# P times V on four quarters of the array, results in the free halves of the score banks, a third accumulator for the feed-forward product, and routing with eight wider matmuls

## Chip, cores and metric

The kernel runs on one core of one Trainium2 chip. The metric is the device time of one execution in microseconds (us); the time before is the median of three runs.

## The reference

Three stages follow one another on 4608 tokens of width 512. Everything is float32, and the kernel keeps that accuracy by splitting each operand into a high and a low float16 half and adding three products (high·high, high·low, low·high).

```
# attention in chunks of 64, 8 heads of width 64
scores = q_c @ k_c.T / sqrt(64);  attn = softmax(scores);  x = attn @ v_c
# dense feed-forward, 512 -> 2048 -> 512
h = relu(x @ w_in);  x = (h * h) @ w_out
# 8 experts, top 1: the router picks one expert for each token
logits = x @ w_gate + modality_bias[modality_id];  e = argmax(logits)
gate = softmax(logits)[e];  out = gate * (relu(x @ w1[e]) @ w2[e])
```

## The kernel before

Tokens are cut into 36 tiles of 128, and four tiles make a super (nine supers). A tile of attention runs through `attn_split` (halves of q and k), `attn_s` (scores, TensorE), `attn_max` (VectorE), `attn_exp` (ScalarE), `attn_p`, `attn_psplit`, `attn_ptr` (a transposing DMA), `attn_pv` (P times V, TensorE), `attn_x` (the result is split into `xt`, its high half on ScalarE, its low half on VectorE), `x_sq` and `x_norm`. For each super, sixteen steps `mm1` (12 matmuls of 512 columns each, into a PSUM tile `hp`) and sixteen steps `mm2` (12 such matmuls, into `op`) follow. ScalarE takes `hp` out as `r`, VectorE squares it to `g`, ScalarE writes the high half of the square into `big`, and GpSimd the low half. After `mm2`, `x2_evac`, `x2_tr`, `route_a` and `route_b` store the row and its expert; the experts' weights are split beside that (`piece_split`). When all tiles are through, slots of 128 rows of one expert each run `slot_mm1` and `slot_mm2`; their rows come by a gather (`slot_gather`) and a transposing DMA (`slot_tr`).

The order on each engine is written by the program itself. For tiles 8 to 35, `attn_events` gives each part of a tile a planned time (`attn_pv` at 36 us of the tile's own plan, `attn_s` at 14, a new tile every 20.5 us of that plan), and `flush` issues what is due before each step of 2.65 planned us; a table `COST` of ScalarE and VectorE time puts parts off when either is too full, and a table `AFTER` holds a part back until an earlier one has been issued. The first 86 us are ordered by `plan_start`, a list of operations with dependencies and due times. Tiles 0 to 3 (`FULL`) multiply in float32 without halves.

PSUM has eight banks: two for `hp` (pool `ps_h`), two for `op`, two for the scores (`s_all`, of which each bank uses columns 0 to 255; at the start `narrow_hi` writes columns 256 to 511 too), one for P times V (`ps_x`) and one for everything small (`ps_r`). In `attn_pv` head half `j` has its operands on partitions 64j, and its result goes to partitions 64j of the one bank:

```
nc.tensor.matmul(xp[h, hp, 64 * c:64 * c + 64], lhsT=vs[h, la, c, hp, :],
                 rhs=pt[h, lb * KD + hp, 64 * c:64 * c + 64], start=n == 0, stop=n == 2)
```

In `attn_s` the four pairs of operand half `j` and result half `c` go to four places: partitions 64c of bank `j`.

`route_a` makes 12 matmuls of 8 columns and VectorE finds the largest logit; ScalarE's exponential of the logits stands at the end of `route_a`, in ScalarE's order ahead of whatever comes next there.

Of the kernel before, what the change touches and what calls it, by code (L numbers as in the profile page):

```python
# [8 lines left out]
F32 = mybir.dt.float32  # L9
F16 = mybir.dt.float16  # L10
# [3 lines left out]
AF = mybir.ActivationFunctionType  # L14
ALU = mybir.AluOpType
# [15 lines left out]
def kernel(  # L31
# [39 lines left out]
    ps_h = ctx.enter_context(tc.tile_pool(name="ps_h", bufs=2, space=bass.MemoryType.PSUM))  # L71
    ps_o = ctx.enter_context(tc.tile_pool(name="ps_o", bufs=2, space=bass.MemoryType.PSUM))
    ps_s = ctx.enter_context(tc.tile_pool(name="ps_s", bufs=1, space=bass.MemoryType.PSUM))
    ps_x = ctx.enter_context(tc.tile_pool(name="ps_x", bufs=1, space=bass.MemoryType.PSUM))
# [35 lines left out]
    wgs = const.tile([128, 2, KD, E], F16, name="wgs")  # L110
# [43 lines left out]
    def consts_c():  # L154
        wg, ids = cb["wg"], cb["ids"]
        act(wgs[:, 0], wg, scale=SWG)
        stt(wgs[:, 1], wg, SWG, wgs[:, 0], ALU.mult, ALU.subtract)
# [31 lines left out]
    s_all = ps_s.tile([128, 2, 512], F32, tag="s", name="s_all")  # L189
    wl = {}  # L190
# [224 lines left out]
    def attn_pv(i):  # L415
        a = at[i]
        pt = a["pt"]
        xp = ps_x.tile([128, KD, 128], F32, tag="x", name="xp")
        a["xp"] = xp
        if i < FULL:  # L420
            for hp in range(KD):
                for c in range(2):
                    for j in range(2):
                        h = slice(64 * j, 64 * j + 64)
                        nc.tensor.matmul(xp[h, hp, 64 * c:64 * c + 64], lhsT=a["vv"][h, c * KD + hp, :],
                                         rhs=pt[h, hp, 64 * c:64 * c + 64], start=True, stop=True)
            return
        vs = a["vs"].rearrange("p l (c h) d -> p l c h d", c=2)
        for hp in range(KD):
            for c in range(2):  # L430
                for n, (la, lb) in enumerate(PASSES):
                    for j in range(2):
                        h = slice(64 * j, 64 * j + 64)
                        nc.tensor.matmul(xp[h, hp, 64 * c:64 * c + 64], lhsT=vs[h, la, c, hp, :],
                                         rhs=pt[h, lb * KD + hp, 64 * c:64 * c + 64], start=n == 0, stop=n == 2)
# [20 lines left out]
    def attn_x(i, part=None):  # L456
        su, t, _, _ = where[i]
        if su not in xts:
            xts[su] = xt_p.tile([128, 2, KD, 512], F16, tag="xt", name="xt")
        a = at[i]  # L460
        x = xts[su]
        sl = slice(t * 128, t * 128 + 128)
        sx = SV if i < FULL else 1.0 / SP_
        if part != 1:
            act(x[:, 0, :, sl], a["xp"], scale=sx)
        if part != 0:
            stt(x[:, 1, :, sl], a["xp"], sx, x[:, 0, :, sl], ALU.mult, ALU.subtract)
# [115 lines left out]
    def route_a(i):  # L583
        a = x2[i]
        lp = ps_r.tile([128, 512], F32, tag="r", name="lp")
        n = 0
        for la, lb in PASSES:
            for kk in range(KD):
                nc.tensor.matmul(lp[:, 0:E], lhsT=a["xt"][:, la * KD + kk, :], rhs=wgs[:, lb, kk, :],
                                 start=n == 0, stop=n == 3 * KD - 1)  # L590
                n += 1
        lg = sm_p.tile([128, E], F32, tag="lg", name="lg")
        stt(lg, lp[:, 0:E], a["ui"][:, 0:1], bias_t[:, i, :], ALU.mult, ALU.add)
        m8 = sm_p.tile([128, 8], F32, tag="m8", name="m8")
# [9 lines left out]
        ex = sm_p.tile([128, E], F32, tag="ex", name="ex")  # L604
        se = sm_p.tile([128, 1], F32, tag="se", name="se")
        act(ex, lg, AF.Exp, bias=nm[:, 0:1], accum_out=se)
        a["oh"], a["se"] = oh, se

    def route_b(i):
# [9 lines left out]
        nc.vector.tensor_tensor(out=run, in0=run, in1=a["oh"], op=ALU.add)  # L619
        mt = sm_p.tile([128, 2], F32, tag="mt", name="mt")  # L620
        nc.gpsimd.tensor_copy(out=mt[:, 0:1], in_=tok[:, i:i + 1])
        ga = sm_p.tile([128, 1], F32, tag="ga", name="ga")
        ts2(ga, a["se"], 1e-9, None, ALU.add)
# [213 lines left out]
    def once(fn, s):  # L837
# [16 lines left out]
        attn_p: (0.0, 1.5), attn_psplit: (0.52, 0.0), attn_x: (0.48, 0.6), x_sq: (0.52, 0.0),  # L854
        x_norm: (0.0, 0.2), piece_split: (0.95, 1.14), x2_evac: (1.2, 1.1), route_a: (0.3, 0.9),
        route_b: (0.0, 0.8),
# [60 lines left out]
    def attn_events(i, a0):  # L917
        more = i + 2 < NTILE
        at_chain([
            (a0 + o, fn, (i + d,)) for o, fn, d in (  # L920
                (0.0, attn_split, 0), (4.5, attn_load, 2), (14.0, attn_s, 0), (16.0, attn_max, 0),
                (18.0, attn_exp, 0), (20.0, attn_p, 0), (23.0, attn_psplit, 0), (23.1, attn_vsplit, 0),
                (26.0, attn_ptr, 0), (27.5, attn_vload, 2), (36.0, attn_pv, 0), (38.0, attn_x, 0), (40.0, x_sq, 0),
                (45.0, x_norm, 0),
            ) if d == 0 or more
        ])
# [5 lines left out]
    def plan_start():  # L932
# [14 lines left out]
        for i in range(FIRST + 2):  # L947
# [14 lines left out]
            else:  # L962
                op(("qh", i), "ACT", 1.05, [("lq", i), ("s", i - 2)], attn_split, i, 0)
                op(("ql", i), "DVE", 1.37, [("qh", i)], attn_split, i, 1)
                op(("s", i), "PE", 0.60, [("ql", i), ("mx", i - 1)], attn_s, i)
# [14 lines left out]
            op(("xh", i), "ACT", 0.60, [("pv", i)], attn_x, i, 0)  # L980
            op(("xl", i), "DVE", 0.69, [("xh", i)], attn_x, i, 1)
# [11 lines left out]
        ops["np", 7][3].append(("onb", KF - 1))  # L993
        op(("cc",), "DVE", 0.60, [("old", KF - 1)], consts_c)
# [79 lines left out]
    for su, (b0, nt, sb) in enumerate(supers):  # L1074
# [7 lines left out]
        for t, qq in M2 if su == 0 else [(t, qq) for t in range(nt) for qq in range(4)]:  # L1082
# [12 lines left out]
            if i == NTILE - 1:  # L1095
                ch += [(T + 12.4, map_b1, ()), (T + 18.4, map_b2, ()), (T + 18.5, once, (slot_w1, EARLY)),
                       (T + 18.6, once, (slot_w2, EARLY)), (T + 21.0, map_b3, ()),
                       (T + 21.1, once, (slot_gather, EARLY)), (T + 21.2, once, (slot_gather, EARLY + 1)),
                       (T + 28.0, once, (slot_tr, EARLY)), (T + 30.0, once, (slot_tr, EARLY + 1))]
# [21 lines left out]
    with tc.manual_schedule():  # L1121
# [3 lines left out]
        for n, (T, fn, a) in enumerate(steps):  # L1125
# [137 lines left out]
```

## Time and profile before

| | |
|---|---|
| median of three runs | 1281.58 us (1281.47 to 1286.59) |
| the profiled execution's own time | 1282.98 us |
| its span, first to last instruction | 1281.3 us |
| TensorE busy | 1232.0 us, 96% of the span |
| VectorE, ScalarE, GpSimd busy | 671.4, 553.8, 409.0 us |
| granted TensorE clock, mean share | 0.989 |

Busy time is time in which at least one instruction of that engine is under way. A matmul's record is longer than the distance to the next one, since they overlap; what a group of matmuls costs TensorE is read from the start of the group to the start of what follows. A bracket in the timeline is the engine's idle time ahead of a row, with what ended it.

### The profile page before, as it was taken

The page shows a single profiled execution, that of the slowest core. Times are in us where ns is not written, and L with a number is a line of the kernel's source. Part 1 is how long each engine was busy: PE and PEld are TensorE (multiplying, and loading weights), DVE is VectorE, ACT ScalarE, POOL GpSimd, SP SyncE. Part 2 cuts the span into 40 slices and gives each one's busy share as a digit, 9 for nine tenths or more (in the row PEclk, how much of TensorE's full clock was granted, in tenths as well). Part 3 has the DMA queues.
Part 4 walks back from the last instruction along what each step waited for, and adds up shares of the span by engine and source line. Part 5 has one row for each costly group of instructions (what it writes and reads, how often), then busy time and mean ns, then how long its engine had stood idle before and what let it go on. Part 6 is the DMA issues. An engine that isn't in the chain of part 4 may idle for free. (4 is left out here: it accounts for less than half of the span.)

```text
span 1281.3 us, 28844 instructions
## 1 busy us (share of the span) xinstructions
PE 1232.0 (96%) x11836; PEld 698.2 (54%) x11836; DVE 671.4 (52%) x1467; ACT 553.8 (43%) x978; POOL 409.0 (32%) x389
## 2 busy tenths in 40 slices
PE   5898999999999999999999999999899999999998
PEld 4443444444444444444444444447677776777775
DVE  6799676796695776776866864514111111111110
ACT  6887564564564554654755653512111111111111
POOL 4487251361350341440531531511222111111111
PEclk8899999999999999999999999999999999999999
DMA  9455536657558458458676553075355337622322
GB/s 375 153 163 167 127 93 188 182 149 218 161 177 218 133 164 223 141 154 217 158 196 175 140 153 111 10 221 164 77 125 102 78 78 259 139 75 75 76 75 59
DMA packets 177867, 190.64 MB, mean 149 GB/s; under 512 B 124876, under 2 KB 124916, under 8 KB 176707
## 3 DMA queue, kind: packets, MB, share of 16 engines
q1 hardware_dynamic: 128930, 157.72, 42.6%
q0 software_dynamic: 7616, 20.80, 5.3%
q10 hardware_dynamic: 41184, 10.23, 4.9%
q8 instruction: 94, 1.54, 0.5%
q14 instruction: 43, 0.34, 0.1%
HBM read 241.02 MB, written 53.08 MB: 230 GB/s over the span
## 5 line engine op out<-in xcount | busy, mean ns | idle before, releaser
L544 PE MATMUL hp<-xt,big 128*128 128x512 f16 x1728 | 388.5, 381 | 9.4 <-ACT r L87 9.2
L559 PE MATMUL op<-big,big 128*128 128x512 f16 x1728 | 384.0, 380 | 0.5 <-POOL big L524 0.5
L544 PEld LDWEIGHTS <-big 128*128 128x128 f16 x1728 | 164.3, 98 | 200.5 <-issue 14.9
L559 PEld LDWEIGHTS <-big 128*128 128x128 f16 x1728 | 165.0, 98 | 193.7 <-issue 1.5
L524 POOL TENSOR_TENSOR big<-g,big 128x512 f16<-128x512 f32 x144 | 176.2, 1227 | 211.9 <-DVE g L90 148.5
L90 DVE SCALAR_TENSOR_TENSOR ht<-hp,ht 128x512 f16<-128x512 f32 x74 | 51.2, 692 | 331.0 <-ACT ht L87 331.0
L812 PEld LDWEIGHTS <-big 128*128 128x128 f16 x3552 | 204.3, 99 | 16.0 <-issue 4.3
L826 PE MATMUL op<-big,ht 128*128 128x512 f16 x888 | 197.6, 379 | 0.0
L812 PE MATMUL hp<-big,big 128*128 128x128 f16 x3168 | 185.5, 221 | 7.4 <-DMA big<-big 3.8
L90 DVE SCALAR_TENSOR_TENSOR g<-r,bq 128x512 f32<-128x512 f32 x138 | 136.4, 993 | 31.7 <-ACT r L87 30.6
L826 PEld LDWEIGHTS <-ht 128*128 128x128 f16 x888 | 85.2, 98 | 96.2
L90 DVE SCALAR_TENSOR_TENSOR wss<-wst,wss 128x1024 f16<-128x1024 f32 x64 | 91.0, 1421 | 62.4 <-ACT wss L87 61.9
L832 POOL DMA_INDIRECT out_dram<-o,tib x33 | 33.5, 1014 | 269.7 <-ACT o L87 250.9
L87 ACT ACTIVATE ht<-hp 128x512 f16<-128x512 f32 x74 | 44.2, 597 | 155.8 <-PE hp L812 155.7
L626 POOL DMA_INDIRECT meta<-mt,di x36 | 41.0, 1138 | 213.5 <-issue 80.8
L87 ACT ACTIVATE big<-r,bls 128x512 f16<-128x512 f32 x138 | 99.4, 721 | 6.4 <-DVE bli L96 0.7
L87 ACT ACTIVATE r<-hp 128x512 f32<-128x512 f32 x138 | 80.9, 586 | 49.3 <-PE hp L544 31.9
L87 ACT ACTIVATE wss<-wst 128x1024 f16<-128x1024 f32 x64 | 67.0, 1047 | 57.2 <-DMA wsp<-wss 39.5
L87 ACT ACTIVATE o<-op,fsb 128x512 f32<-128x512 f32 x33 | 22.7, 687 | 153.3 <-PE op L826 153.3
L407 POOL TENSOR_TENSOR ps<-ee,ps 128x512 f16<-128x512 f32 x32 | 44.1, 1380 | 89.4 <-ACT ps L87 88.0
L87 ACT ACTIVATE ex<-lg,nm 128x8 f32<-128x8 f32 x36 | 10.8, 301 | 116.2 <-DVE nm L94 116.2
L90 DVE SCALAR_TENSOR_TENSOR qkt<-qk,qkt 128x1024 f16<-128x1024 f32 x32 | 44.3, 1383 | 12.8 <-ACT qkt L87 12.0
(175 smaller groups left out, 1008.1 us busy)
## 6 DMA issues: line engine op xcount, KB each, us to landing
big<-wsp SPq DMA_DIRECT2D x72, 2048.0 KB
wst<-in_w_dram SPq DMA_DIRECT2D x64, 512.0 KB
wsp<-wss SPq DMA_DIRECT2D x64, 512.0 KB
qk<-in_qk_dram SPq DMA_DIRECT2D x36, 512.0 KB
vv<-in_v_dram SPq DMA_DIRECT2D x36, 256.0 KB
x2d<-xs SPq DMA_DIRECT2D x36, 256.0 KB
big<-in_w_in_dram SPq DMA_DIRECT2D x16, 512.0 KB
wl<-in_w_out_dram SPq DMA_DIRECT2D x16, 512.0 KB
```

What stands on the lines that cost most here:

```text
L87: nc.scalar.activation(out=out, in_=in_, func=func, **kw)
L90: nc.vector.scalar_tensor_tensor(out=out, in0=in0, scalar=s, in1=in1, op0=op0, op1=op1, **kw)
L407: nc.gpsimd.tensor_tensor(out=a["ps"][:, 1], in0=pf, in1=a["ps"][:, 0], op=ALU.subtract)
L524: nc.gpsimd.tensor_tensor(out=lo, in0=q32.rearrange("p (f n) -> p f n", f=nf), in1=hi, op=ALU.subtract)
L544: nc.tensor.matmul(hp[:, q_ * n:(q_ + 1) * n], lhsT=wi[:, la, kk, f * 128:f * 128 + 128], rhs=x[:, lb, kk, :], start=i == 0, stop=i == 3 * ...
L559: nc.tensor.matmul(ps, lhsT=g[:, la, f, t * 128:t * 128 + 128], rhs=wo[:, lb, f, :], start=f == 0 and n == 0, stop=f == KF - 1 and n == 2)
L626: nc.gpsimd.indirect_dma_start(out=meta[:, :], out_offset=bass.IndirectOffsetOnAxis(ap=di[:, 0:1].bitcast(U32), axis=0), in_=mt, in_offset ...
L812: nc.tensor.matmul(hp[:, f4 * 128:f4 * 128 + 128], lhsT=w[:, la, kk, f * 128:f * 128 + 128], rhs=xt[:, lb * KD + kk, :], start=n == 0, sto ...
L826: nc.tensor.matmul(ps, lhsT=ht[:, la, f, :], rhs=w[:, lb, f, :], start=f == 0 and n == 0, stop=f == KF2 - 1 and n == 2)
L832: nc.gpsimd.indirect_dma_start(out=out[:, :], out_offset=bass.IndirectOffsetOnAxis(ap=slot[s][0].bitcast(U32), axis=0), in_=o, in_offset=N ...
```

## The change

- `attn_pv` for tiles 4 to 35 puts its result into columns 256 to 511 of the score banks: operand half `j` into bank `j`, result half `c` on partitions 64c, with `c` and `j` as the inner loops, so that the four quarters of the array take turns. Tiles 0 to 3 take a buffer of `ps_h` instead of `ps_x`.
- The bank of `ps_x` goes to `ps_h`, which has three buffers; `mm1` may have three results waiting instead of two.
- `attn_x` takes the four quarters out one by one: four instructions on ScalarE and four on VectorE of 64 partitions by 256 elements, in place of one and one of 128 by 512.
- `route_a` makes 8 matmuls of 16 columns (high and low half of the weights side by side, so that the product low·low is added too) and VectorE adds the two halves of the logits in two instructions. The exponential moves to `route_b`, between VectorE's instructions there.
- In the order: `attn_pv` 36 to 43, `attn_x` 38 to 45.5, `x_sq` 40 to 48, `x_norm` 45 to 51; the costs of `attn_x` and the routing; in the start plan, `s(i)` waits for the low half of tile i−2's result and `pv(i)` for the maximum of tile i+1. `slot_tr` for the first two slots after the early ones comes 4 us earlier in its chain.

```diff
-    ps_h = ctx.enter_context(tc.tile_pool(name="ps_h", bufs=2, space=bass.MemoryType.PSUM))
+    ps_h = ctx.enter_context(tc.tile_pool(name="ps_h", bufs=3, space=bass.MemoryType.PSUM))
...
-    ps_x = ctx.enter_context(tc.tile_pool(name="ps_x", bufs=1, space=bass.MemoryType.PSUM))
...
+    xps = [s_all[:, c, 256:512].rearrange("p (h n) -> p h n", h=KD) for c in range(2)]
...
-            for c in range(2):
-                for n, (la, lb) in enumerate(PASSES):
+            for n, (la, lb) in enumerate(PASSES):
+                for c in range(2):
                     for j in range(2):
                         h = slice(64 * j, 64 * j + 64)
-                        nc.tensor.matmul(xp[h, hp, 64 * c:64 * c + 64], lhsT=vs[h, la, c, hp, :],
+                        o = 64 * c
+                        nc.tensor.matmul(xps[j][o:o + 64, hp, :], lhsT=vs[h, la, c, hp, :],
                                          rhs=pt[h, lb * KD + hp, 64 * c:64 * c + 64], start=n == 0, stop=n == 2)
...
+        for j in range(2):
+            for c in range(2):
+                sl = slice(t * 128 + 64 * c, t * 128 + 64 * c + 64)
+                xp, h = xps[j][64 * c:64 * c + 64], slice(64 * j, 64 * j + 64)
+                if part != 1:
+                    act(x[h, 0, :, sl], xp, scale=1.0 / SP_)
+                if part != 0:
+                    stt(x[h, 1, :, sl], xp, 1.0 / SP_, x[h, 0, :, sl], ALU.mult, ALU.subtract)
...
-        n = 0
-        for la, lb in PASSES:
-            for kk in range(KD):
-                nc.tensor.matmul(lp[:, 0:E], lhsT=a["xt"][:, la * KD + kk, :], rhs=wgs[:, lb, kk, :],
-                                 start=n == 0, stop=n == 3 * KD - 1)
-                n += 1
+        for kk in range(2 * KD):
+            nc.tensor.matmul(lp[:, 0:2 * E], lhsT=a["xt"][:, kk, :], rhs=wgs[:, kk % KD].rearrange("p l e -> p (l e)"),
+                             start=kk == 0, stop=kk == 2 * KD - 1)
         lg = sm_p.tile([128, E], F32, tag="lg", name="lg")
         stt(lg, lp[:, 0:E], a["ui"][:, 0:1], bias_t[:, i, :], ALU.mult, ALU.add)
+        stt(lg, lp[:, E:2 * E], a["ui"][:, 0:1], lg, ALU.mult, ALU.add)
...
-        act(ex, lg, AF.Exp, bias=nm[:, 0:1], accum_out=se)
-        a["oh"], a["se"] = oh, se
+        a["oh"], a["nm"], a["lg"] = oh, nm, lg
...
         nc.vector.tensor_tensor(out=run, in0=run, in1=a["oh"], op=ALU.add)
...
+        act(ex, a["lg"], AF.Exp, bias=a["nm"][:, 0:1], accum_out=se)
...
-        ts2(ga, a["se"], 1e-9, None, ALU.add)
+        ts2(ga, se, 1e-9, None, ALU.add)
...
-        attn_p: (0.0, 1.5), attn_psplit: (0.52, 0.0), attn_x: (0.48, 0.6), x_sq: (0.52, 0.0),
+        attn_p: (0.0, 1.5), attn_psplit: (0.52, 0.0), attn_x: (1.4, 1.5), x_sq: (0.52, 0.0),
...
-                (26.0, attn_ptr, 0), (27.5, attn_vload, 2), (36.0, attn_pv, 0), (38.0, attn_x, 0), (40.0, x_sq, 0),
-                (45.0, x_norm, 0),
+                (26.0, attn_ptr, 0), (27.5, attn_vload, 2), (43.0, attn_pv, 0), (45.5, attn_x, 0), (48.0, x_sq, 0),
+                (51.0, x_norm, 0),
...
-                op(("s", i), "PE", 0.60, [("ql", i), ("mx", i - 1)], attn_s, i)
+                op(("s", i), "PE", 0.60, [("ql", i), ("mx", i - 1), ("xl", i - 2)], attn_s, i)
...
+        for i in range(FULL, FIRST - 1):
+            ops["pv", i][3].append(("mx", i + 1))
...
-                       (T + 28.0, once, (slot_tr, EARLY)), (T + 30.0, once, (slot_tr, EARLY + 1))]
+                       (T + 24.0, once, (slot_tr, EARLY)), (T + 26.0, once, (slot_tr, EARLY + 1))]
...
-            while (fn is mm1 and len(pend) == 2) or (pend and fn is mm2 and (a[0] or a[1] < 2)) or any(x not in done for x in need):
+            while (fn is mm1 and len(pend) == 3) or (pend and fn is mm2 and (a[0] or a[1] < 2)) or any(x not in done for x in need):
```

## Rows read from the trace of the kernel before

**Rows 1.** The page's part 1: busy us, share of the span, instructions.

```profile
PE 1232.0 (96%) x11836; PEld 698.2 (54%) x11836; DVE 671.4 (52%) x1467; ACT 553.8 (43%) x978; POOL 409.0 (32%) x389
```

**Rows 2.** Waits of TensorE, whole span: us in total, times, longest us.

```profile
PE hp L544 <- ACT r L87: 9.2, 10, 1.9
...
PE hp L812 <- DMA big<-big: 3.8, 1, 3.8
...
PE xp L434 <- DVE xt L90: 3.1, 1, 3.1
...
PE xp L434 <- issue: 2.5, 1, 2.5
```

**Rows 3.** Groups by form, TensorE: xcount | busy us, mean ns | idle.

```profile
L434 PE MATMUL xp<-pt,vs 64*64 64x64 f16 x1536 | 30.7, 195 | 5.7 <-DVE xt L90 3.1 <-issue 2.5
...
L353 PE MATMUL s_all<-qkt 64*64 64x64 f16 x1536 | 18.6, 195 | 0.3 <-DVE ee L366 0.3
```

**Rows 4.** Timeline of TensorE, 350 to 372 us: start, us, what.

```profile
358.97 0.94 PE L434 MATMUL xp<-pt,vs 64*64 64x64 f16 x48
359.85 2.76 PE L544 MATMUL hp<-xt,big 128*128 128x512 f16 x12
...
370.36 0.58 PE L353 MATMUL s_all<-qkt 64*64 64x64 f16 x48
370.87 1.47 PE L544 MATMUL hp<-xt,big 128*128 128x512 f16 x6
```

**Rows 5.** Timeline of TensorE, 422 to 448 us.

```profile
430.25 0.45 PE L589 MATMUL lp<-wgs,x2t 128*128 128x8 f16 x12
430.56 2.75 PE L544 MATMUL hp<-xt,big 128*128 128x512 f16 x12
435.17 2.75 PE L544 MATMUL hp<-xt,big 128*128 128x512 f16 x12 [1.86 <-ACT r L87]
```

**Rows 6.** Timeline of ScalarE, 422 to 448 us.

```profile
434.24 0.30 ACT L87 ACTIVATE ex<-lg,nm 128x8 f32<-128x8 f32 x1 [5.03 <-DVE nm L94]
...
434.54 0.57 ACT L87 ACTIVATE r<-hp 128x512 f32<-128x512 f32 x1
```

**Rows 7.** Timeline of TensorE, 860 to 925 us: two slots' first product.

```profile
901.27 5.54 PE L812 MATMUL hp<-xgt,big 128*128 128x128 f16 x96
...
915.80 7.15 PE L812 MATMUL hp<-big,big 128*128 128x128 f16 x96 [3.82 <-DMA big<-big]
```

**Rows 8.** Timeline of ScalarE and its DMA issues, 872 to 925 us.

```profile
912.07 0.69 ACT L87 ACTIVATE o<-op,fsa 128x512 f32<-128x512 f32 x1 [4.63 <-PE op L826]
912.40 2.75 ACTq L797 DMA_TRANSPOSE big<-big  x2
```

**Rows 9.** Timeline of GpSimd in the same stretch: the second slot's gather.

```profile
904.75 0.97 POOL L785 DMA_INDIRECT big<-x2d,tib  x1 [0.30 <-issue]
```

**Rows 10.** Groups by form, ScalarE.

```profile
L87 ACT ACTIVATE xt<-xp 128x512 f16<-128x512 f32 x36 | 20.9, 582 | 5.5 <-PE xp L434 5.1 <-PE xp L425 0.4
...
L87 ACT ACTIVATE wgs<-wg 128x32 f16<-128x32 f32 x1 | 0.2, 218 | 0.0
```

**Rows 11.** Groups by form, VectorE.

```profile
L90 DVE SCALAR_TENSOR_TENSOR xt<-xp,xt 128x512 f16<-128x512 f32 x36 | 24.6, 684 | 5.2 <-ACT xt L87 5.2
...
L90 DVE SCALAR_TENSOR_TENSOR lg<-lp,ui,bias_t 128x8 f32<-128x8 f32 x36 | 8.0, 221 | 16.2 <-PE lp L589 16.2
```

**Rows 12.** Timeline of all engines, 0 to 45 us: a score matmul.

```profile
14.24 1.13 PE L345 MATMUL s_all<-qk 64*64 64x64 f32 x32 [2.59 <-DVE big L90]
```

**Rows 13.** Busy time by stretch: PE, PEld, DVE, ACT, POOL, clock, DMA.

```profile
80.00:130.00 50.00, 43.44 (x462) 21.33 (x461) 47.13 (x68) 39.13 (x72) 40.51 (x34) 0.98 0.58 174
...
200.00:760.00 560.00, 551.61 (x4982) 266.34 (x4981) 407.48 (x875) 308.98 (x543) 190.95 (x169) 1.00 0.64 176
```

**Rows 14.** Timeline of VectorE, 358 to 379 us.

```profile
365.65 0.68 DVE L90 SCALAR_TENSOR_TENSOR xt<-xp,xt 128x512 f16<-128x512 f32 x1
...
376.55 0.69 DVE L366 TENSOR_TENSOR ee<-s_all,mx 128x512 f32<-128x512 f32 x1
```

More of the change, by code (lines that the diff above doesn't have):

```diff
@@ L109 @@
     run = const.tile([128, E], F16, name="run")
-    wgs = const.tile([128, 2, KD, E], F16, name="wgs")
+    wgs = const.tile([128, KD, 2, E], F16, name="wgs")
     wnorm = const.tile([128, 1], F32, name="wnorm")
@@ L155, in consts_c @@
         wg, ids = cb["wg"], cb["ids"]
-        act(wgs[:, 0], wg, scale=SWG)
-        stt(wgs[:, 1], wg, SWG, wgs[:, 0], ALU.mult, ALU.subtract)
+        act(wgs[:, :, 0], wg, scale=SWG)
+        stt(wgs[:, :, 1], wg, SWG, wgs[:, :, 0], ALU.mult, ALU.subtract)
         idf = st_p.tile([128, 2 * DM], F16, tag="xs", name="idf", bufs=4)[:NTILE, 0:256].bitcast(F32)
@@ L417, in attn_pv @@
         pt = a["pt"]
-        xp = ps_x.tile([128, KD, 128], F32, tag="x", name="xp")
-        a["xp"] = xp
         if i < FULL:
+            xp = ps_h.tile([128, 512], F32, tag="h", name="xp").rearrange("p (k n) -> p k n", k=KD)
+            a["xp"] = xp
             for hp in range(KD):
@@ L462, in attn_x @@
         sl = slice(t * 128, t * 128 + 128)
[L463 to L467, printed above, removed]
+        if i < FULL:
+            if part != 1:
+                act(x[:, 0, :, sl], a["xp"], scale=SV)
+            if part != 0:
+                stt(x[:, 1, :, sl], a["xp"], SV, x[:, 0, :, sl], ALU.mult, ALU.subtract)
+            return
+        for j in range(2):
+            for c in range(2):
+                sl = slice(t * 128 + 64 * c, t * 128 + 64 * c + 64)
+                xp, h = xps[j][64 * c:64 * c + 64], slice(64 * j, 64 * j + 64)
+                if part != 1:
+                    act(x[h, 0, :, sl], xp, scale=1.0 / SP_)
+                if part != 0:
+                    stt(x[h, 1, :, sl], xp, 1.0 / SP_, x[h, 0, :, sl], ALU.mult, ALU.subtract)
     def x_sq(i):
@@ L603, in route_a @@
         ts2(nm, m8[:, 0:1], -1.0, None, ALU.mult)
-        ex = sm_p.tile([128, E], F32, tag="ex", name="ex")
-        se = sm_p.tile([128, 1], F32, tag="se", name="se")
-        act(ex, lg, AF.Exp, bias=nm[:, 0:1], accum_out=se)
-        a["oh"], a["se"] = oh, se
+        a["oh"], a["nm"], a["lg"] = oh, nm, lg
     def route_b(i):
@@ L619, in route_b @@
         nc.vector.tensor_tensor(out=run, in0=run, in1=a["oh"], op=ALU.add)
+        ex = sm_p.tile([128, E], F32, tag="ex", name="ex")
+        se = sm_p.tile([128, 1], F32, tag="se", name="se")
+        act(ex, a["lg"], AF.Exp, bias=a["nm"][:, 0:1], accum_out=se)
         mt = sm_p.tile([128, 2], F32, tag="mt", name="mt")
@@ L853 @@
         attn_split: (0.95, 1.14), attn_vsplit: (1.04, 1.2), attn_max: (0.0, 1.2), attn_exp: (0.52, 0.0),
-        attn_p: (0.0, 1.5), attn_psplit: (0.52, 0.0), attn_x: (0.48, 0.6), x_sq: (0.52, 0.0),
-        x_norm: (0.0, 0.2), piece_split: (0.95, 1.14), x2_evac: (1.2, 1.1), route_a: (0.3, 0.9),
-        route_b: (0.0, 0.8),
+        attn_p: (0.0, 1.5), attn_psplit: (0.52, 0.0), attn_x: (1.4, 1.5), x_sq: (0.52, 0.0),
+        x_norm: (0.0, 0.2), piece_split: (0.95, 1.14), x2_evac: (1.2, 1.1), route_a: (0.0, 0.9),
+        route_b: (0.3, 0.8),
     }
@@ L979, in plan_start @@
                 op(("pv", i), "PE", 0.94, [("pt", i), ("vl", i), ("xl", i - 1)], attn_pv, i)
-            op(("xh", i), "ACT", 0.60, [("pv", i)], attn_x, i, 0)
-            op(("xl", i), "DVE", 0.69, [("xh", i)], attn_x, i, 1)
+            op(("xh", i), "ACT", 0.60 if i < FULL else 1.50, [("pv", i)], attn_x, i, 0)
+            op(("xl", i), "DVE", 0.69 if i < FULL else 1.50, [("xh", i)], attn_x, i, 1)
             op(("sq", i), "ACT", 0.90, [("xh", i)], x_sq, i)
```

## Prediction

> **What bounds the kernel now.** The page's busy times come first: TensorE is busy 1232.0 of 1281.3 us, no other engine over 671.4 [rows 1]. So TensorE's own time is the time, and two things can shorten it: fewer TensorE microseconds in a group of matmuls, or fewer waits ahead of one. Second, the view of waits: TensorE's largest are 9.2 us, ten times, for ScalarE to take a first product out of `hp`, and 3.8 us for a transposed slot; at the start P times V waits 3.1 us for VectorE and 2.5 us more [rows 2]. Third, the groups by form: P times V and the scores are 1536 matmuls of the same shape each, yet cover 30.7 us against 18.6 [rows 3]. Last, the timelines around these waits and the busy time by stretch, which say what is behind each wait and how much room VectorE has.
>
> **The change part by part.**
>
> *P times V on four quarters.* One tile's 48 matmuls hold TensorE from 358.97 to 359.85, 0.88 us; the 48 of the scores, whose four halves already take turns over four quarters and two banks, from 370.36 to 370.87, 0.51 us [rows 4]. The new order has the scores' places and shapes, so I take their price: 0.37 us less on each of 32 tiles, **−11.8 us**. The bounds are that and nothing (if it is the operands and not the quarters that make P times V slow).
>
> *Routing.* Twelve matmuls hold TensorE from 430.25 to 430.56, 0.31 us [rows 5]. Eight at the same pace take 0.21: 0.10 on 36 tiles, **−3.7 us**. Sixteen columns instead of eight could cost a little of it; the least is nothing. VectorE gets a second small instruction like the one of 221 ns [rows 11], 36 times, 8 us beside TensorE's work.
>
> *The exponential and the third accumulator.* The waits for `hp` have one pattern. At 434.24 ScalarE begins the exponential after 5.03 us in which it waited for VectorE's routing; `r` comes out of `hp` only behind it, at 434.54 [rows 6], and TensorE, which had waited 1.86 us, goes on at 435.17 [rows 5]. With the exponential in `route_b`, two steps later, its input is old when ScalarE comes to it. And a third buffer lets TensorE make one more product, 2.75 us by its record [rows 5], which is more than the longest of these waits, 1.9 [rows 2]. Either alone would do: **−9.2 us**; at least half must go, since the third buffer needs nothing else. In exchange VectorE waits in `route_b` until ScalarE reaches the exponential; behind it stand `g` and the splits, which TensorE needs only steps later.
>
> *`slot_tr` earlier.* The two transposes are issued at 912.40, because in ScalarE's order they stand behind an eviction that waited 4.63 us for TensorE and began at 912.07 [rows 8]; the last gather that they need had been issued by 905.7 [rows 9]. The slot's product begins at 915.80 after 3.82 us, and its 96 matmuls take 7.15 us instead of 5.54 [rows 7]. Issued 4 us earlier, they would stand ahead of that eviction. All of it is worth 3.8 + 1.6 = 5.4 us, none of it nothing (if the gather lands late); near the top, **−4.0 us**.
>
> *Taking the result out in four pieces.* ScalarE takes 582 ns for 512 elements and 218 for 32 [rows 10]; on that line 256 take 0.39 us, four 1.55, so 0.97 us more for each tile. VectorE by 684 and 221 ns [rows 11]: 0.45 each, 1.80 for four, 1.12 more, 36 us on 32 tiles. From 200 to 760 us VectorE is busy 407 of 560 us [rows 13], 73%; 24 tiles there bring it to about 79% with the routing. That is hidden behind the matmuls as long as nothing on TensorE waits for it.
>
> *New waits on the shared banks.* But now something does. A score matmul wrote columns 0 to 255 of `s_all`, and waited 2.59 us for VectorE, which read columns 256 to 511 [rows 12]: the halves of these banks are ordered as one. So P times V of tile i waits until the maximum of tile i+1 has been read, if that was issued ahead of it, and the scores of tile i+2 wait for the last piece of tile i's result. Behind either wait stand all matmuls. In the trace, tile 17's product was at 358.97, its result out at 366.33 [rows 14], and tile 19's scores at 370.36 [rows 4]: 4.0 us to spare. The new plan moves the product 7 us later and lengthens the taking out by 1.5 to 2.7 us; so the two meet. Where the taking out is issued after those scores, nothing waits; just ahead, the scores wait for what is left of it, 1 to 3 us. The other order is like it: the scores of 370.36 are read out by 377.24 [rows 14], and a product issued in those 6.3 us waits 2 to 5. Since the order is by steps of 2.65 planned us, and the meeting shifts from tile to tile, I count a wait of some 1.2 us for every third tile: **+12 us**, 0.4 us for each of about 30 tiles. The bounds are nothing and 1.5 us for each tile, 48 us.
>
> The pieces' length depends on whether VectorE's reading of one half of the partitions holds up ScalarE's reading of the other: 0.39 + 1.80 = 2.2 us for all if not, 4 × (0.39 + 0.45) = 3.4 if so. The trace has only reads on all 128 partitions, so it cannot say. The Trainium skill (PSUM — Partial Sum Buffer, section "PSUM bank collisions raise a hardware error") says that two engines collide in a bank only within the same quadrant of 32 partitions. By that the halves need no order, and the bank waits would be the smaller, about 8 us instead of 12, with a sum of 1265; no run here shows it yet.
>
> *The start.* From 80 to 130 us VectorE is busy 47.1 of 50 us and TensorE idle 6.6 [rows 13], mostly the two waits of P times V [rows 2]. Four tiles bring VectorE 4 × 1.12 = 4.5 us more there, and scores, maximum, product and result of tiles 4 to 7 now follow one another. TensorE's saving there (1.5 us) is in the sum already. **+4 us**, between 0 (TensorE's idle time takes it) and 10 (the 4.5, and waits like the 3.1 and 2.5 once more).
>
> *Sum.* −11.8 − 3.7 − 9.2 − 4.0 + 12 + 4 = −12.7 on the span of 1281.3: 1268.6. The profiled execution's own time is 1282.98, 1.7 above its span and 1.4 above the median, so the median lies 0.3 above the span: **1269 us**.
>
> **The rivals.** 0.5% is about what a measurement of this kernel can tell from no change: faster is below 1275.2, slower above 1288.0.
>
> *The cover holds.* The order happens to keep products and scores apart, as in the tile above with 4 us; bank waits 2 us, nothing at the start: 1281.3 − 28.7 + 2 + 0.3 = 1255. For it: scores are spaced by some 20 us and each stay in the banks is 3 to 7. Against it: the meeting point is where the plan now puts them.
>
> *The waits eat the gain.* The same waits at 0.7 to 0.9 us for each tile: 22 to 29 us, 1279 to 1286, no change.
>
> *Slower: the banks become the bound.* Each piece waits for the other engine's piece, ScalarE and VectorE are both held 3.4 us for each tile, VectorE's queue grows, and each tile makes TensorE wait 1.5 us: 1281.3 − 28.7 + 4 + 48 + 0.3 = 1305. It decides from (28.7 − 4)/32 = 0.77 us for each tile. For it: VectorE is the second busiest engine, and reads a maximum 6 us late even now [rows 14]. Against it: the exponential's waits go from ScalarE. The Trainium skill (TensorEngine Tiling (Array Packing), section "PSUM Bottleneck") warns of this: packing speeds up TensorE, not the taking out of PSUM, which may become the bottleneck. The busy times so far speak for room.
>
> *Four quarters are not faster.* P times V stays at 0.88 us: 1269 + 11.8 = 1281. Against it: the scores, of the same shape, take 0.51.
>
> **How the numbers follow.** Forecast (1259 to 1275): 0.49. Cover holds: 0.15. Waits eat the gain: 0.19. Quarters no faster: 0.05. Slower: 0.12. So faster 0.64, same 0.24, slower 0.12. A range from 1254 to 1287 leaves out the slower case and a third of the case in which the cover holds, 0.17 together.
>
> **What would show it.** A tile's P times V should hold TensorE about 0.51 us, the routing 0.21; the waits of `hp` for ScalarE should be under 2 us in all; the slot's product should begin without its 3.8 us. In their place TensorE's waits should name VectorE's maximum ahead of `xp` and its `xt` ahead of the scores, some 12 us together, over the span. The prediction is wrong if these are near 0 or over 25, if P times V keeps its 0.88, or if the feed-forward product of a super waits for its last tile's late result, which the later plan brings nearer and which I have not priced.

## The result and the profile after

The changed kernel takes 1300.74 us (median of 4 runs, 1294.39 to 1302.93), beside 1281.53 of the kernel before on the same chip: 1.013 of before, 95% interval 1.0095 to 1.0165. It is slower by 1.3%, where 1269 us was forecast. The profiled execution took 1302.93 us, its span is 1301.2, 19.9 above that of before, and the mean granted clock 0.977 (0.989 before).

The page's part 1 answers to [rows 1]:

```profile
PE 1224.8 (94%) x11692; PEld 684.8 (53%) x11692; DVE 700.5 (54%) x1599; ACT 584.6 (45%) x1074; POOL 417.8 (32%) x389
```

TensorE is busy 7 us less and the span is 20 us longer: most of the loss is idle time. The rest is hidden in the busy time, where P times V and the routing fell by 15 us (30.7 to 18.9 and 16.0 to 12.6): the first feed-forward products rose by 5 us (388.5 to 393.9), since some of them ran at the slower clock. The groups by form (busy us, mean ns, idle ahead of them) answer to [rows 3]:

```profile
L554 PE MATMUL hp<-xt,big 128*128 128x512 f16 x1728 | 393.9, 386 | 2.9 <-ACT xt L86 2.9
...
L353 PE MATMUL s_all<-qkt 64*64 64x64 f16 x1536 | 19.0, 197 | 12.4 <-DVE xt L89 12.4
L435 PE MATMUL s_all<-pt,vs 64*64 64x64 f16 x1536 | 18.9, 196 | 5.6 <-DVE ee L366 3.1 <-DVE xt L89 2.4
L597 PE MATMUL lp<-wgs,x2t 128*128 128x16 f16 x288 | 12.6, 170 | 11.4 <-DMA x2t<-xs 11.4
```

P times V (L435) now covers 18.9 us, as the scores do (L353), in place of 30.7: that is what the four quarters promised. But each of these groups now has idle time ahead of it. The waits of TensorE (us in total, times, longest) answer to [rows 2]:

```profile
PE s_all L353 <- DVE xt L89: 12.4, 8, 3.8
PE lp L597 <- DMA x2t<-xs: 11.4, 2, 10.8
PE hp L820 <- DMA big<-wsp: 9.8, 1, 9.8
PE idp L164 <- DVE wl L89: 4.9, 1, 4.9
PE s_all L435 <- DVE ee L366: 3.1, 1, 3.1
PE hp L554 <- ACT xt L86: 2.9, 1, 2.9
PE s_all L435 <- DVE xt L89: 2.4, 2, 1.3
PE rp L618 <- DVE nm L93: 2.5, 4, 0.8
```

The waits for `r` (9.2 us) and for the slot's transposed rows (3.8) are gone, as forecast. Scores and product wait 17.9 us for the banks that they now share. Two long waits stand there that the prediction didn't price: the routing's 10.8 us for its transposed input, and 9.8 us for expert weights (3.6 before).

The 10.8 us are worth following, in the timeline of all engines (start, us, what, the idle time ahead):

```profile
421.88 9.25 PE L554 MATMUL hp<-xt,big 128*128 128x512 f16 x36 [2.88 <-ACT xt L86]
...
430.96 0.35 PE L597 MATMUL lp<-wgs,x2t 128*128 128x16 f16 x8
...
431.35 0.23 DVE L89 SCALAR_TENSOR_TENSOR lg<-lp,ui,bias_t 128x8 f32<-128x8 f32 x1 [3.91 <-PE lp L597]
...
431.98 0.36 PE L491 MATMUL np<-xn,ones_f 128*128 128x4 f32 x2 [0.68 <-DVE lg L89]
...
433.62 0.72 ACT L86 ACTIVATE big<-r,bls 128x512 f16<-128x512 f32 x1 [6.34 <-DVE bli L95]
...
440.30 0.67 DVE L380 TENSOR_REDUCE sum<-ee 128x8 f32<-128x512 f32 x1
...
442.18 0.63 ACT L86 ACTIVATE ps<-ee 128x512 f16<-128x512 f32 x1 [4.13 <-DVE ee L385]
...
444.06 1.23 SPq L412 DMA_TRANSPOSE pt<-ps  x1
...
445.97 1.23 SPq L589 DMA_TRANSPOSE x2t<-xs  x1
...
449.70 0.38 PE L597 MATMUL lp<-wgs,x2t 128*128 128x16 f16 x8 [10.77 <-DMA x2t<-xs]
```

Tile 19, the last of its super, is taken out so late that the super's first product waits 2.88 us for it. Its norm stands behind three steps of `mm1` in TensorE's order, so ScalarE, which needs the norm's scale, stands still for 6.34 us. VectorE comes to the next tile's sum at 440.30, ScalarE to its `ps` at 442.18, and SP can issue the transpose of that `ps` only at 444.06, when GpSimd has written its low half. The routing's transpose, whose rows were ready at 426.0, stands behind it in SP's queue. From 420 to 460 us (the columns are: stretch, length, busy time of PE, PEld, DVE, ACT, POOL, granted clock, DMA) it looks like this in the kernel before,

```profile
420.00:460.00 40.00, 37.28 (x331) 17.84 (x330) 32.23 (x65) 24.84 (x43) 19.54 (x17) 1.00 0.55 159
```

and like this after, with 200 to 760 us, which answers to [rows 13], as the second row:

```profile
420.00:460.00 40.00, 26.07 (x165) 11.50 (x165) 24.73 (x65) 19.98 (x39) 10.91 (x11) 0.79 0.44 136
...
200.00:760.00 560.00, 530.18 (x4718) 249.22 (x4716) 411.38 (x945) 321.25 (x594) 191.43 (x163) 0.98 0.61 170
```

Beside the waits the clock falls: 0.79 of full over this stretch, part of it at the lower of the two levels (half of full from 441.6 to 455.3 us). This one super holds most of the loss: from its first product to that of the next super 108.5 us pass (421.9 to 530.4), and 93.7 before (418.9 to 512.6), while at the first product of the super ahead of it, at 328.2 and 328.4, the two kernels were level. And the pieces of a tile's result go out like this, in the same timeline:

```profile
418.86 0.38 ACT L86 ACTIVATE xt<-s_all 64x256 f16<-64x256 f32 x1 [2.21 <-DVE ee L366]
419.27 0.42 DVE L89 SCALAR_TENSOR_TENSOR xt<-s_all,xt 64x256 f16<-64x256 f32 x1 [0.50 <-ACT xt L86]
419.72 0.38 ACT L86 ACTIVATE xt<-s_all 64x256 f16<-64x256 f32 x1 [0.48 <-DVE xt L89]
420.13 0.43 DVE L89 SCALAR_TENSOR_TENSOR xt<-s_all,xt 64x256 f16<-64x256 f32 x1 [0.45 <-ACT xt L86]
```

ScalarE's second piece waits until VectorE has read the first, and so on: 0.86 us a pair, 3.4 for a tile, the upper of the two lengths that the prediction left open.

### The profile page after: what moved, and what is told of

It reads as the page before. It is cut to its first block, busy times and chain, and to the rows that moved or that the text cites. A ratio compares the mean times of both kernels' runs of the same rounds, so it can differ in the third digit from the quotient of the medians.

```text
span 1301.2 us, 28794 instructions
## 1 busy us (share of the span) xinstructions
PE 1224.8 (94%) x11692; PEld 684.8 (53%) x11692; DVE 700.5 (54%) x1599; ACT 584.6 (45%) x1074; POOL 417.8 (32%) x389
## 5 line engine op out<-in xcount | busy, mean ns | idle before, releaser
L554 PE MATMUL hp<-xt,big 128*128 128x512 f16 x1728 | 393.9, 386 | 2.9 <-ACT xt L86 2.9
L534 POOL TENSOR_TENSOR big<-g,big 128x512 f16<-128x512 f32 x144 | 183.4, 1278 | 206.8 <-DVE g L89 157.1
L820 PEld LDWEIGHTS <-big 128*128 128x128 f16 x3552 | 203.4, 98 | 18.5 <-DMA big<-wsp 10.8
L89 DVE SCALAR_TENSOR_TENSOR g<-r,bq 128x512 f32<-128x512 f32 x138 | 130.3, 952 | 33.5 <-ACT r L86 28.4
L89 DVE SCALAR_TENSOR_TENSOR wss<-wst,wss 128x1024 f16<-128x1024 f32 x64 | 86.8, 1357 | 34.0 <-ACT wss L86 33.3
L86 ACT ACTIVATE xt<-s_all 64x256 f16<-64x256 f32 x128 | 48.0, 375 | 86.0 <-DVE xt L89 75.6
L89 DVE SCALAR_TENSOR_TENSOR xt<-s_all,xt 64x256 f16<-64x256 f32 x128 | 53.8, 420 | 39.9 <-ACT xt L86 39.8
```

What stands on the lines that cost most here:

```text
L86: nc.scalar.activation(out=out, in_=in_, func=func, **kw)
L89: nc.vector.scalar_tensor_tensor(out=out, in0=in0, scalar=s, in1=in1, op0=op0, op1=op1, **kw)
L534: nc.gpsimd.tensor_tensor(out=lo, in0=q32.rearrange("p (f n) -> p f n", f=nf), in1=hi, op=ALU.subtract)
L554: nc.tensor.matmul(hp[:, q_ * n:(q_ + 1) * n], lhsT=wi[:, la, kk, f * 128:f * 128 + 128], rhs=x[:, lb, kk, :], start=i == 0, stop=i == 3 * ...
L820: nc.tensor.matmul(hp[:, f4 * 128:f4 * 128 + 128], lhsT=w[:, la, kk, f * 128:f * 128 + 128], rhs=xt[:, lb * KD + kk, :], start=n == 0, sto ...
```

## Experiments

They ran on other chips, on which the kernel before takes 1283 to 1290 us, so each is told by its ratio to the kernel before on its own chip. In e1 to e12 short gaps of some 0.5 us (one of 1.1 in e6) ahead of the expert products ("issue") add up to 3.8 to 5.1 us; they stand in e1 and e8 too, which keep the old product, and are no part of the question. Since the expert stage differs so from run to run, profiles of two chips are compared only up to its start, which e1 and e8 reach at 855.5 and 855.7 us; they differ only in two transposes that come behind it.

**e1, the routing and the exponential alone, in the kernel before.**

```
-    for la, lb in PASSES: ... 12 matmuls of 8 columns
+    for kk in range(2 * KD): ... 8 matmuls of 16 columns
-    act(ex, lg, AF.Exp, ...)      # in route_a
+    act(ex, a["lg"], AF.Exp, ...) # in route_b
```

> The kernel before with the routing of the changed kernel alone (8 matmuls of 16 columns, the exponential in route_b); P times V, banks, plan and slot_tr as before. Theory A (the routing's part of the forecast is sound and the loss sits in the shared banks and the later plan): the routing's matmuls cost 3.4 us less, the 9.2 us in which TensorE waits for hp go to under 3, time 1268 to 1273. Rival B (the exponential only carries its wait over to VectorE, and the loss of the changed kernel comes from there): hp waits or others stay at 6 to 12 us, time 1277 to 1290.

0.9936 (0.9913 to 0.9960). The routing covers 8.1 us in place of 11.3, and TensorE's list has no wait for `r`, with two accumulators:

```profile
PE hp L810 <- DMA big<-wsp: 9.7, 1, 9.7
PE hp L810 <- DMA big<-big: 4.1, 1, 4.1
```

So those 9 us go without a third accumulator; the exponential was not moved alone. By ratio the time is at the edge of what the first theory said (1273 us on the first chip). The wait for expert weights is 9.7 us here too, in a kernel that the change of P times V doesn't touch: over all runs it is 3.6 to 10.3 us, and the 6 us more in the profile after can't be laid to the change.

**e2, the loops of the taking out exchanged**, so that ScalarE's next piece lies in the other bank.

```
-        for j in range(2):
-            for c in range(2):
+        for c in range(2):
+            for j in range(2):
```

> The changed kernel with the two loops of attn_x exchanged, so that one piece after another is in the other bank: ScalarE need not wait for VectorE, taking a tile out should last 2.2 us instead of 3.5. Theory A (waits on the shared banks are the larger loss, and they are the length of taking out): scores waiting for xt fall from 12.4 to under 6 us, time 1290 to 1296. Rival B (the later plan is the larger loss: late last tile, late norm, and the routing that waits 11 us for its transposing DMA): the time stays at 1297 to 1303, whatever the bank waits do.

1.0141 (1.0103 to 1.0179). The pieces alternate as before:

```profile
419.81 0.38 ACT L86 ACTIVATE xt<-s_all 64x256 f16<-64x256 f32 x1 [0.48 <-DVE xt L89]
420.67 0.38 ACT L86 ACTIVATE xt<-s_all 64x256 f16<-64x256 f32 x1 [0.48 <-DVE xt L89]
```

Neither other partitions nor another bank frees ScalarE. What is ordered is the whole of `s_all`. The scores' wait stays too (12.7 us), so the run doesn't decide between its two theories.

**e3, the plan times of the kernel before.**

```
-  (43.0, attn_pv, 0), (45.5, attn_x, 0), (48.0, x_sq, 0), (51.0, x_norm, 0)
+  (36.0, attn_pv, 0), (38.0, attn_x, 0), (40.0, x_sq, 0), (45.0, x_norm, 0)
```

> The changed kernel with the planned times of before for attn_pv, attn_x, x_sq and x_norm (36, 38, 40, 45). Theory A (bank waits): they stay, at 12 to 25 us, since products now meet the maximum of the next tile more often; time 1293 to 1303. Rival B (the later plan): hp waiting for xt (2.9 us) and the routing waiting for its transposing DMA (11.4 us) go, and the scores keep more distance from the result; time 1275 to 1288.

1.0303 (1.0264 to 1.0342): worse than either theory said. The routing's long wait is gone, but the banks cost

```profile
PE s_all L353 <- DVE xt L89: 30.8, 6, 7.3
PE s_all L435 <- DVE ee L366: 5.4, 4, 2.2
```

**e4, two accumulators** (`ps_h` with 2 buffers, two results pending).

```
-    ps_h ... bufs=3    ;  len(pend) == 3
+    ps_h ... bufs=2    ;  len(pend) == 2
```

> The changed kernel with two accumulators instead of three (the eighth bank is left unused). Theory A (with the exponential moved, the third accumulator carries nothing): within 0.4% of the changed kernel, 1296 to 1305. Rival B (it catches ScalarE's new waits): TensorE waits for hp by 5 to 15 us, time 1305 to 1315.

1.0094 (1.0068 to 1.0120). Waits for `r` come back, 5.2 us; the routing's 10.8 us go. Tile 19 is as late as before, since the super's first product waits 2.88 us for it here too. What differs is SP's order: with `flush` running in other places, the routing's transpose is issued ahead of that of `ps`.

```profile
423.38 7.03 PE L554 MATMUL hp<-xt,big 128*128 128x512 f16 x24 [2.88 <-ACT xt L86]
...
429.87 2.20 SPq L589 DMA_TRANSPOSE x2t<-xs  x1
...
451.34 1.54 SPq L412 DMA_TRANSPOSE pt<-ps  x1
```

So the late tile alone doesn't make the routing's long wait; its place behind a blocked transpose does. The third accumulator earns nothing here that the time shows; it was not run beside the old place of the exponential.

**e9, tile 19 alone planned 8 us earlier.**

```
-        attn_events(i, A0[i])
+        attn_events(i, A0[i] - (8.0 if i == 19 else 0.0))
```

> The kernel after with one number changed: the whole chain of tile 19 (the last tile of the fifth feed-forward block) is planned 8 us earlier, so that its result is issued four steps ahead of the first product that reads it, as in the kernel before, and not in the same step. Theory A (the wait of 10.8 us of the routing for its transposed input, and the 2.9 us of the first product ahead of it, come from this one late tile, through a blocked ScalarE and the DMA queue): both go, the bank waits stay near 18 us, and the time falls by 13 to 16 us, to 1.000 to 1.004 of before. Rival (the queue is late anyway, because the pieces hold ScalarE and VectorE 3.5 us a tile): a wait of 5 us or more of the routing or of a first product is found near 420 to 450 us, and the time stays above 1.008.

1.0139 (1.0109 to 1.0169): no gain. The wait of the routing and that of the first product are gone, and the scores wait 26.2 us in place of 12.4. My theory that without them 13 to 16 us are won falls, though a gain of a few us would lie within the interval. Of the new waits 5.8 us stand in the same stretch, the longest 280 us later, where the edit has shifted the order; that the one wait turned into the other isn't shown. At both, ScalarE's second piece waits while VectorE is in a routing. Here is the first, and then the longest with its pieces:

```profile
440.41 0.86 PE L353 MATMUL s_all<-qkt 64*64 64x64 f16 x48 [5.81 <-DVE xt L89]
...
719.54 0.36 ACT L86 ACTIVATE xt<-s_all 64x256 f16<-64x256 f32 x1
...
721.01 0.21 DVE L89 SCALAR_TENSOR_TENSOR lg<-lp,ui,bias_t 128x8 f32<-128x8 f32 x1
...
723.15 0.14 DVE L93 TENSOR_SCALAR nm<-m 128x1 f32<-128x1 f32 x1
723.21 0.40 DVE L89 SCALAR_TENSOR_TENSOR xt<-s_all,xt 64x256 f16<-64x256 f32 x1
723.65 0.38 ACT L86 ACTIVATE xt<-s_all 64x256 f16<-64x256 f32 x1 [3.75 <-DVE xt L89]
...
726.27 0.86 PE L353 MATMUL s_all<-qkt 64*64 64x64 f16 x48 [8.20 <-DVE xt L89]
726.44 0.60 ACT L86 ACTIVATE r<-hp 128x512 f32<-128x512 f32 x1
```

ScalarE has begun the taking out; VectorE is in the middle of a routing. ScalarE can't go on to its second piece, and for 3.75 us it does nothing else either: `r`, which TensorE's products need, is next at 726.44. Four times in each tile the two engines must be there together.

**e6, four ScalarE pieces first, then four VectorE pieces.**

```
+        for q in (0, 1) if part is None else (part,):
             for j in range(2):
                 for c in range(2):
-                    if part != 1: act(...)    # and at once: if part != 0: stt(...)
+                    act(...) if q == 0 else stt(...)
```

> The kernel after, with the eight pieces of a tile's result issued as four on ScalarE and then four on VectorE. The banks are held about as long (4 x 0.38 + 4 x 0.42 = 3.2 us for 3.5), but neither engine waits between its pieces: ScalarE's waits for VectorE ahead of xt, 75.6 us over 84 instructions, should all but go. Theory A (TensorE waits for the banks, and how long the two engines are held costs nothing): the waits of the scores for xt stay at 10 to 13 us and the time at 1.010 to 1.015 of before. Rival (the two engines held 3.5 us a tile delay everything behind them): the time falls to 1.003 or under, and the waits of the scores below 8 us.

0.9975 (0.9957 to 0.9994), so 1.5% under the kernel after: the rival. The banks are held hardly less (411.85 to 415.16, 3.3 us), but each engine goes through its part at a stretch:

```profile
411.85 1.55 ACT L86 ACTIVATE xt<-s_all 64x256 f16<-64x256 f32 x4 [2.48 <-DVE ee L366]
...
413.43 1.73 DVE L89 SCALAR_TENSOR_TENSOR xt<-s_all,xt 64x256 f16<-64x256 f32 x4 [1.68 <-ACT xt L86]
```

The scores' wait falls from 12.4 to 4.9 us, though the routing still waits 8.9: that wait doesn't need the alternation.

**e7, two tiles of one bank each**, taken out bank by bank (two ScalarE pieces, then two VectorE pieces), maximum and subtraction once for each bank, which costs VectorE 11 us more in all (60.6 for 49.5). The narrowing of weights at the start uses the whole first bank in this kernel and overwrites scores of the first tiles, so it serves for its time alone.

```
-    s_all = ps_s.tile([128, 2, 512], F32, tag="s", ...)
+    s_b = [ps_s.tile([128, 512], F32, tag="s%d" % c, ...) for c in range(2)]
```

> The kernel after with the two score banks as two tiles of one bank each, and the result taken out bank by bank (two ScalarE pieces, then two VectorE pieces, of each); the maximum becomes two reductions and two subtractions of half the size. Theory A (the pieces alternate because the program orders all accesses to a tile, here two banks, one after the other): ScalarE is on the second bank while VectorE is on the first, and a tile's result is out after 2.3 to 2.6 us in place of 3.5; the bank waits fall from 17.9 us to about 12, and the time to about 1.007 of before. Rival (the two engines can't read at once whatever the tiles are): 3.4 us as before, and 1.012 or more, since the maximum costs VectorE some 0.3 us more a tile.

0.9969 (0.9953 to 0.9985).

```profile
411.23 1.56 ACT L86 ACTIVATE xt<-s_b 64x256 f16<-64x256 f32 x4 [1.68 <-DVE ee L368]
...
412.04 1.73 DVE L89 SCALAR_TENSOR_TENSOR xt<-s_b,xt 64x256 f16<-64x256 f32 x4
```

The two engines work side by side and the result is out after 2.54 us: the order was that of the tile. The waits at the banks are 7.3 us, the routing's 10.6 remain. The time is that of e6: what the 0.8 us less in the banks bring, net of VectorE's 11 us, can't be measured.

**e5 and e12, the order held apart.** `flush` holds the scores of tile i back until three steps after the taking out of tile i−2, and the product of tile i until three steps after the maximum of tile i+1. The kernel of e5 has the order of e6 as well, which its expectation left unsaid; e12 has the rule alone.

```
+            if fn is attn_s and n is not None and n - at_n.get((attn_x, a[0] - 2), -9) < 3 or (
+                    fn is attn_pv and n is not None and n - at_n.get((attn_max, a[0] + 1), -9) < 3):
+                kept.append(e)
+                continue
```

> The kernel after with one more rule when the plan's work is issued: the scores of tile i stay back until at least three steps of TensorE after the taking out of tile i-2, and the product of tile i until at least three steps after the maximum of tile i+1; nothing else changes. Theory A (the loss is the order on the shared banks, with the slow clock that follows each wait): the waits for xt and ee ahead of scores and product fall from 17.9 us to under 5, TensorE's excess on the slow clock from 16 us to about 11, and the time to 0.985 to 0.995 of before. Theory B (the loss is the later plan: last tiles, norms and routing late): the bank waits fall too, but waits of mm1 and of the routing take their place, and the time stays above 1.005 of before.

> The kernel after with the rule of e5 alone (scores and product held back by three steps), and the pieces alternating between ScalarE and VectorE as in the kernel after. Theory A (the order of issue is what costs, not the length of the taking out): bank waits under 6 us after 131 us, 0.986 to 0.991 of before. Rival (both are needed, since engines held 3.5 us a tile delay what follows): 0.994 to 1.002, with waits of first products or of the routing for ScalarE's and VectorE's results.

e5: 0.9871 (0.9839 to 0.9903), with 7.9 us at the banks, where under 5 was expected, and no wait of the routing's product. e12: 1.0017 (0.9998 to 1.0037), its rival. With alternating pieces the waits only change their place:

```profile
PE s_all L435 <- DVE ee L366: 10.0, 3, 5.8
...
PE s_all L435 <- DVE xt L89: 4.7, 3, 2.0
PE s_all L353 <- DVE xt L89: 4.6, 2, 2.3
```

So both count. The order of the pieces brings 1.5%, the rule 1.1% without it and 1.0% on top of it.

**e11, e5 with the plan times of before** (the edit of e3).

> The kernel of e5 with the plan times of the kernel before (product at 36, result at 38, squares at 40, norm at 45). With the old times and no rule the scores waited 30.8 us for the result. Theory A (only the distance between scores, result and maximum in the order of issue decides, not the plan times): bank waits under 6 us after 131 us, and 0.985 to 0.990 of before. Rival (the later plan is needed as well): the held scores come late, the waits move to first products or to ee, and the time is 0.995 or more.

0.9867 (0.9843 to 0.9890), that of e5. With both repairs the later plan is of no use; without them the old times stood 3.0% above the kernel before (e3), the later ones 1.3%.

**e8, the routing, the exponential and the earlier `slot_tr`, in the kernel before.** e1 and

```
-  (T + 28.0, once, (slot_tr, EARLY)), (T + 30.0, once, (slot_tr, EARLY + 1))
+  (T + 24.0, once, (slot_tr, EARLY)), (T + 26.0, once, (slot_tr, EARLY + 1))
```

> The kernel before with the routing product in eight matmuls, the exponential in the second routing step and the two late slot transposes 4 us earlier; product of P and V, accumulators and plan as before. Theory A (these parts give what the prediction said, each by itself): 3.7 + 9.2 + 4.0 less, so 0.987 to 0.990 of before; the wait of the slot's first product for its transposed rows, 3.8 us, is gone. Rival (the slot's product waits then for the second layer's weights or a late gather instead): 0.993 to 0.994, as with the routing alone.

0.9862 (0.9829 to 0.9895); the wait for `big<-big` is gone.

**e10, e5 with tiles 4 to 7 as before the change.**

```
-        if i < FULL:     # own bank, taken out whole
+        if i < FIRST:    # the same for tiles 4 to 7, on two diagonal quarters
```

The start plan loses the two conditions and the longer costs that the change had given it.

> The kernel of e5 (issue held back by three steps, and four ScalarE pieces ahead of four VectorE pieces), with tiles 4 to 7 as before the change: their product on two diagonal quarters into a bank of its own, taken out whole. Theory A (the start lost some 4 us to the shared banks and the longer taking out): the waits of 2.3, 4.9 and 1.3 us before 131 us fall to some 3.9 in all, and the time is 3 to 5 us under e5's 0.987, at 0.983 to 0.985 of before. Rival (VectorE's work at the start sets the time whatever the banks): 0.986 to 0.988.

0.9862 (0.9840 to 0.9885), the rival: the start's waits are those of before (3.1 and 2.5 us), the gain over e5 is within the interval.

**e13, the quarters undone in all tiles of e10; e14, e10 with four and five steps in place of three.**

```
e13:  -        if i < FIRST:     +        if i < NTILE:
e14:  -  (attn_x ...) < 3 ; (attn_max ...) < 3     +  ... < 4 ; ... < 5
```

> The kernel of e10 with the quarters undone in all tiles: the product of P and V on two diagonal quarters, into a bank of its own of the three that the first products use, and taken out whole (one ScalarE and one VectorE instruction); rule of issue, plan and routing as in e10. Theory A (with the bank waits gone the quarters give the 11.8 us that the prediction counted, so this kernel lacks them): 1280 us or 0.994 of before, 0.8% above e10, with P times V at 28 us of TensorE. Rival (on the shared banks what the quarters save is used up by the longer taking out and the slow clock behind the waits that remain): the time is within 0.3% of e10's 0.986, with fewer waits ahead of product and scores and less excess on the slow clock.

> The kernel of e10 with the scores held back until four steps after the result of tile i-2, and the product until five steps after the maximum of tile i+1 (three and three in e10). Theory A (what remains of the bank waits, 3.8 + 1.0 + 1.0 us ahead of the product, is still too small a distance): these go, and the time falls to 0.981 to 0.984 of before. Rival (holding back makes the last tiles of a feed-forward block late, whose results now come 2.7 to 5.3 planned us ahead of their first reader, in place of 5 to 10): the waits move to the first products and the routing, and the time is 0.987 or more.

e13: 0.9850 (0.9824 to 0.9876), the rival. Its 1260.41 us are the shortest median of the study, but on a faster chip; by ratio it can't be told from e5, e8, e10 and e11. P times V covers its old 28.2 us again, yet nothing is lost by it. TensorE's whole list from 44 us on:

```profile
PE hp L832 <- DMA big<-wsp: 5.1, 2, 3.2
PE xp L428 <- DVE xt L89: 3.1, 1, 3.1
PE op L581 <- POOL big L546: 0.5, 1, 0.5
PE s_all L353 <- DVE ee L366: 0.3, 1, 0.3
```

e14: 0.9947 (0.9932 to 0.9963), the rival's time, though the waits are other ones than it named: held back further, the product waits 10.9 us for the maximum and a norm waits 4.3 us.

## Why the prediction was wrong

The 19.9 us between the two spans, beside the prediction's terms. What a group costs is read from start to start; "slow clock" is what is left of the distances between large matmuls beyond those at full clock (0.216 us for 512 columns, 0.056 for 128).

| term | predicted | measured |
|---|---|---|
| P times V on quarters | −11.8 | −12.0 (28.4 to 16.4) |
| routing, eight matmuls | −3.7 | −3.4 (11.3 to 7.9) |
| waits for `r` | −9.2 | −9.2 |
| earlier `slot_tr` | −4.0 | −3.8 |
| start, 44 to 135 us | +4 | +4.4 (2.3 idle, 2.1 slow clock) |
| waits on the shared banks after it | +12 | +14.4 (10.1 scores, 4.3 product) |
| routing product, its counts and the norm, first products: waits for late work | not priced | +18.1 (10.5 + 4.7 + 2.9) |
| slow clock, 135 to 894 us | not priced | +5.9 |
| expert stage beside `slot_tr` | 0 | +5.7 |

The first six come to −9.6; the prediction had −12.7. It is the last three, +29.7, that turn the result; 0.2 us is left over in small ones. Of these the expert stage's is the spread that e1 showed. The failed step is **new waits on the shared banks**, the +12 us: it counted how long TensorE stands at the two banks, and that part was nearly right (nine waits after the start, 14.4 us, in place of every third tile at 1.2 us), but it put at nothing what else the sharing does. ScalarE and VectorE must both come to a tile four times, each standing idle until the other is there (ScalarE 75.6 us in all ahead of `xt`), and the order that this and the later plan make lets the routing, the norm and first products wait for late work, 18.1 us, with 5.9 us of slow clock beside it. None of these waits stands in e8, which has neither the shared banks nor the later plan. That VectorE's longer work is "hidden behind the matmuls as long as nothing on TensorE waits for it" was right for the work and wrong for the waiting. The prediction named the super that waits for its last tile as a danger and didn't price it. That super is where most was lost; e4 shows that the largest wait in it, the routing's, hangs on SP's order, and e9, which takes the late tile away, gains nothing that the time shows.

Of the rivals, *the banks become the bound* had half of the mechanism: pieces that alternate, 3.4 us a tile, both engines held. Its own price, 1.5 us for each tile at the banks, was too high by a factor of three. e6 shows what the alternation costs: without it the kernel is 1.5% faster, with the banks held nearly as long. The other half is the order of issue, 1.0 to 1.1% (e12, and e5 against e6), and with both mended the kernel is at 0.987. How the 18.1 us divide between the two causes isn't shown: the routing's wait outlives the alternation (8.9 us in e6, 10.6 in e7) and is gone under the rule of issue alone (e12).

The length of the taking out was left between 2.2 and 3.4 us. The Trainium skill (PSUM — Partial Sum Buffer, section "PSUM bank collisions raise a hardware error") asks for an order only between accesses of two engines to the same bank within the same quadrant of 32 partitions. This program is stricter: it orders the whole two-bank tile (e2 against e7). Whether the halves of one bank could be read at once was not run here.

The plan: that the later times bring the two meetings together was half right. With the old times the banks cost 30.8 + 5.4 us (e3); the later plan was the smaller evil.

Last, the prediction took the quarters' 11.8 us as a gain to be reduced by some waits. In the best order found here they earn nothing that can be measured: e10 and e13 are at 0.9862 and 0.9850, and in the profiles they reach the expert stage at 855.9 and 856.7 us. Up to there TensorE saves 10.3 us on P times V in e10 (28.2 to 17.9) and waits 8.4 us more ahead of product and scores (12.0 against 3.6). Of these, 5.9 us stand ahead of products that go to the shared banks; the other 2.5 are at a tile that runs on diagonal quarters in both kernels, as before, and are no cost of the quarters. So up to some 3 us may be left of the gain, less than these runs can tell from nothing. The Trainium skill (TensorEngine Tiling (Array Packing), section "PSUM Bottleneck") warned that packing doesn't speed up the taking out of PSUM; the trace agrees, with 0.58 us on ScalarE for one piece of 512 elements [rows 10] against 1.55 for four.

What stays open: the quarters with a result that is taken out whole. Both operand halves would then write the same partitions of one bank; it wasn't tried, and no run shows what would come of it. Nor was anything but the order of issue tried against e10's last waits.

## What to carry to other kernels

A result that is taken out in pieces which two engines must read in turn costs not the pieces' time alone but the longer of two queues at every piece; let one engine finish all of its pieces before the other begins, or give each bank a tile of its own. When two users share a buffer, price what stands behind the engines that free it, and not only the wait at the buffer; taking away one wait of such a chain may only show the next. And try the small parts of a large change alone: here the routing with its moved exponential and the earlier transpose gave all of the gain (0.986), and the large part, as it was first ordered, took it back.

## Hardware behaviour not expected

- 64x64 matmuls that take turns over four quarters start 8.4 ns apart, against 16.3 ns on two diagonal quarters, with the same operands (16.4 and 28.4 us for 1536 of them, the steps to the next work included).
- A piece of 64 partitions by 256 elements takes 375 ns on ScalarE and 420 ns on VectorE, so half the partitions save next to nothing: the prediction's estimate for 256 elements, from rows on all 128 partitions (32 and 512 elements on ScalarE, 8 and 512 on VectorE), was 390 and 450.
- Around two waits of TensorE, 2.9 and 10.8 us, that end 28 us apart, the granted clock was 0.79 over 40 us (1.00 before), and in all the slow clock cost 16.3 us, 8.8 before.
